# Two-layer MLP behind a 2-D Fourier transform: the tiles that TensorE reads are laid at one address modulo 256 bytes

## The chip, the cores and the metric

The kernel runs on one core of one Trainium2 chip. A core has five engines that run side by side: TensorE (matmuls, PE in the rows, and PEld for its weight loads), VectorE (DVE), ScalarE (ACT), GpSimd (POOL) and SyncE (SP, which issues the DMAs here). The metric is the device time of one execution in microseconds, lower is better. The on-chip memory that engines read their operands from is called SBUF here; an address is a byte offset within each of its 128 partitions.

## The reference

The reference takes the real part of a 2-D Fourier transform of each of 8 sequences (3008 x 256) and feeds every row to a two-layer network with a squared ReLU.

```python
X = np.fft.fft(x, axis=1)            # x: (8, 3008, 256)
X = np.fft.fft(X, axis=2)
attn = X.real.astype(np.float32)     # rows become 24064 tokens of 256
...
h = x @ w_in                         # 256 -> 2048
r = np.maximum(h, 0.0)
g = s * (r * r) + b
return (g @ w_out).astype(np.float32)  # 2048 -> 256
```

## The kernel before

The transform along the sequence is split into small cosine and sine transforms (L652), and the one along the features is folded into the first layer's weights at the start of the program. What is left as the bulk of the work are the two layers.

The tokens are cut into 8 sequences x 3 blocks (`su`, `blk`) of 502 columns (`NT`), each with a plus and a minus half, so that a tile which TensorE streams has two halves of 502 columns. The 2048 hidden features are cut into 16 chunks `j` of 128. One step is one `j` of one block; there are 8 x 3 x 16 = 384 of them.

Every operand is kept as a high and a low float32r part, and a product is formed from three matmuls (high x high, high x low, low x high):

- **First layer** (L823, function `first_layer`): for each half, three matmuls stream `spec_h`, `spec_l`, `spec_h` against the weights `wd_h`, `wd_h`, `wd_l`. That is 6 matmuls in a step, 2,304 in all.
- VectorE adds a rank-one term and forms sum and difference (L826 to L828), ScalarE squares and casts into `gh` (L842 to L844), and GpSimd (VectorE in some steps) writes the rest `gl = h - gh` (L848).
- **Second layer** (L865, function `second_layer`): for each half `pm`, 6 matmuls stream `gh` and `gl` against `wo_h` and `wo_l`, each for two groups of 128 outputs (`dh`). That is 12 matmuls in a step, 4,608 in all.

Each of these 6,912 matmuls has 128 rows of weights of its own to load. Both layers accumulate in PSUM; `finish` evacuates four banks once in a block.

The order of all this work on every engine is written out by hand, in the two strings `START` (first sequence) and `BATCH` (the other seven): `L` is a first-layer step, `S` a second-layer step, `l`, `v` and `o` are pieces of the next sequence's transform. `_in_order` ties each engine's instructions to that order.

Tiles come from pools, which lie one behind another in SBUF in the order in which they are opened; within a pool, tiles lie in the order in which their tags first appear. `Ring` hands out numbered tags in turn. The pool `const` holds the weights, the pool `read` all that TensorE streams in the two layers (`gl`, `gh`, `spec_l`, `spec_h`, three buffers each). The element lengths given to `tile` thus set the addresses. In the built program they are, in bytes (and modulo 256):

| tile | first byte | first half, modulo 256 | second half, modulo 256 |
|---|---|---|---|
| `wd_h`, `wd_l` | 16640, 33024 | 0 | 0 (8192 bytes on) |
| `wo_h`, `wo_l` | 49472, 65856 | 64 | weights of `j`, `dh` are 1024 and 512 bytes apart, so 64 throughout |
| `gl`, three buffers | 155520, 159616, 163712 | 128 | 96 (2016 bytes on) |
| `gh`, three buffers | 167808, 171904, 176000 | 128 | 96 (2016 bytes on) |
| `spec_l`, three buffers | 180160, 184256, 188352 | 192 | 152 (2008 bytes on) |
| `spec_h`, three buffers | 192704, 196800, 200896 | 192 | 152 (2008 bytes on) |

Some lengths are padded for the layout's sake: the last of the eight first input tiles by 16 elements, one of the `spec_l` buffers by 64.

Of the kernel before, what the change touches and what calls it, by code (L numbers as in the profile page):

```python
# [9 lines left out]
F32 = mybir.dt.float32  # L10
I32 = mybir.dt.int32
F32R = mybir.dt.float32r
# [3 lines left out]
P = 128  # L16
NB, S, D, FF = 8, 3008, 256, 2048
# [3 lines left out]
R = 96  # L21
G = 24
NL = 4 * G
NK = H + 2
NT = 502
NBLK = 3
NJ = FF // P
ENGINES = tuple(getattr(mybir.EngineType, e) for e in ("PE", "DVE", "Activation", "Pool", "SP"))
# [19 lines left out]
TILES = (4, 6, 5, 7, 0, 1, 2, 3)  # L48
# [220 lines left out]
def kernel(ctx: ExitStack, tc: tile.TileContext, xq, xn, dft, turn, feat, w_in, w_out, s, b, out):  # L269
    nc = tc.nc  # L270
# [3 lines left out]
    const = ctx.enter_context(tc.tile_pool(name="const", bufs=1))  # L274
    stage = Ring(ctx.enter_context(tc.tile_pool(name="stage", bufs=1)), 2)
    wst = Ring(ctx.enter_context(tc.tile_pool(name="wst", bufs=1)), 4)
    fold = ctx.enter_context(tc.tile_pool(name="fold", bufs=1))
    small = Ring(ctx.enter_context(tc.tile_pool(name="small", bufs=1)), 2)
    read = Ring(ctx.enter_context(tc.tile_pool(name="read", bufs=1)), 3)
    act = Ring(ctx.enter_context(tc.tile_pool(name="act", bufs=1)), 3)  # L280
    outp = Ring(ctx.enter_context(tc.tile_pool(name="outp", bufs=1)), 2)
    late = ctx.enter_context(tc.tile_pool(name="late", bufs=1))
# [6 lines left out]
    def two_banks():  # L289
        held = banks.take()  # L290
        return held, ps_ab.tile([P, 2, 512], F32, name="ab", tag=f"ab{held[0]}")
# [8 lines left out]
    sb_b = const.tile([P, 1], F32, name="sb_b")  # L300
    turn_sb = const.tile([R, 8], F32, name="turn_sb")
    bias = const.tile([P, 2], F32, name="bias")
    wd_h = const.tile([P, 2, FF], F32R, name="wd_h")
    wd_l = const.tile([P, 2, FF], F32R, name="wd_l")
    wny = const.tile([P, NJ], F32, name="wny")
    wo_h = const.tile([P, NJ, D], F32R, name="wo_h")
    wo_l = const.tile([P, NJ, D], F32R, name="wo_l")
    feat_sb = small.tile([P, 4 * P + 152], F32, name="feat_sb", tag="ebc")[:, :4 * P].rearrange("p (k n) -> p k n", k=2)
# [137 lines left out]
    def nyquist(ph, t, room):  # L446
# [64 lines left out]
        yield  # L511
        e = room if ph else outp.tile([P, 2 * NT], F32, name="e", tag="o")
        to = 0
# [17 lines left out]
    def block_of(su, blk):  # L531
        if (su, blk) not in spec_tiles:
            spec_tiles[su, blk] = [spec_part(part) for part in "hl"]
        return spec_tiles[su, blk]

    def spec_part(part, more=0):
        t = read.tile([P, 1024 + more], F32R, name=f"spec_{part}")
        return t[:, :2 * NT].rearrange("p (k n) -> p k n", k=2)

    folded = {}  # L540

# [75 lines left out]
    def store(su, ph, parts, low_engine=nc.gpsimd):  # L617

        pieces = []
        for r, o in parts:  # L620
            at, groups, size, kept = PLACES[ph][r]
            n = groups * kept
            first = at // NT
            if (at + n - 1) // NT == first:
                pieces.append((
                    first, at - first * NT, n, lambda v, g=groups: v.rearrange("p k (a g) -> p k a g", a=g),
                    o.rearrange("p k (a g) -> p k a g", a=groups)[:, :, :, :kept],
                ))
            else:
                cut = (first + 1) * NT - at  # L630
                pieces.append((first, NT - cut, cut, lambda v: v, o[:, :, :cut]))
# [184 lines left out]
    def first_layer(su, blk, j, ebc):  # L816
        mh, ml = block_of(su, blk)
        held, ps = two_banks()
        ps = ps[:, :, :NT]
        fj = slice(j * P, (j + 1) * P)  # L820
        for kind in range(2):
            for i, (w, m) in enumerate(((wd_h, mh), (wd_h, ml), (wd_l, mh))):
                nc.tensor.matmul(ps[:, kind], w[:, kind, fj], m[:, kind], start=i == 0, stop=i == 2)  # L823
        yield
        h = act.tile([P, 2, NT], F32, name="h")
        nc.vector.scalar_tensor_tensor(h[:, 0], ebc, wny[:, j:j + 1], ps[:, 0], op0=ALU.mult, op1=ALU.add)  # L826
        sub(h[:, 1], h[:, 0], ps[:, 1])  # L827
        add(h[:, 0], h[:, 0], ps[:, 1])  # L828
        banks.give(held)
        step = (su * NBLK + blk) * NJ + j  # L830
        rows = (slice(1, 2), slice(0, 1)) if step in HALVED else (slice(0, 2),)
        gh = read.tile([P, 2, NT + 2], F32R, name="gh")
        gl = read.tile([P, 2, NT + 2], F32R, name="gl")
        if (su, blk) == (0, 0):

            nc.gpsimd.memset(gh[:, 0, NT:].bitcast(F32), 1.0)
            nc.gpsimd.memset(gl[:, 0, NT:].bitcast(F32), 0.0)
        for pm in rows:
            if step in SQUARES_OF_STEPS_ON_VECTOR:
                nc.vector.scalar_tensor_tensor(h[:, pm], h[:, pm], 0.0, h[:, pm], op0=ALU.max, op1=ALU.mult)  # L840
            else:
                nc.scalar.activation(h[:, pm], h[:, pm], AF.Relu)  # L842
                nc.scalar.activation(h[:, pm], h[:, pm], AF.Square)  # L843
            nc.scalar.copy(gh[:, pm, :NT], h[:, pm])  # L844
        yield gh, gl
        engine = nc.vector if step in LOWS_OF_STEPS_ON_VECTOR else nc.gpsimd
        for pm in rows:
            engine.tensor_sub(gl[:, pm, :NT], h[:, pm], gh[:, pm, :NT].bitcast(F32))  # L848
        yield
# [20 lines left out]
    def finish(su, blk, po):  # L870
        if (su, blk) == (0, 0):
            for dh in range(2):
                nc.vector.tensor_scalar(bias[:, dh:dh + 1], po[dh][:, NT:NT + 1], sb_b, None, ALU.mult)
        last = (su, blk) == (NB - 1, NBLK - 1)
        for pm in range(2):
# [15 lines left out]
    tiles = {}  # L891
    for n, c in enumerate(TILES):
        pool, tag = ((stage, "xt"), (read, "gl"), (read, "gh"))[(n + 1) // 3]
        more = 16 if n == len(TILES) - 1 else 0
        t = pool.tile([R, 4 * D + more], F32, name="xt", tag=tag)
        tiles[c] = t[:, :4 * D].rearrange("p (q d) -> p q d", q=4)

    unit = read.tile([P, 1024], F32, name="unit", tag="spec_l")
    minus = unit[:R, 2 * R:6 * R].rearrange("p (i l) -> p i l", i=4)
    lo = [spec_part("l", 64 * k) for k in range(2)]  # L900
    room = read.tile([P, 1024], F32, name="room", tag="spec_h")
    hi = [spec_part("h") for _ in range(2)]
    for k in range(2):
        spec_tiles[0, k] = [hi[k], lo[k]]
# [49 lines left out]
    def load_e(n):  # L954
        su, blk = divmod(n, NBLK)
        ebc[n] = small.tile([P, NT], F32, name="ebc")
        for ph in range(2):
            first, last = max(0, blk * NT - SPLIT * ph), min((blk + 1) * NT - SPLIT * ph, e_dram[ph].shape[1])
            if first < last:
                at = first + SPLIT * ph - blk * NT  # L960
                nc.sync.dma_start(ebc[n][:, at:at + last - first], e_dram[ph][su, first:last].partition_broadcast(P))

    def first():
        nonlocal step
        su, blk, j = step // (NBLK * NJ), step // NJ % NBLK, step % NJ
        step += 1
        n = su * NBLK + blk
        if j == NJ // 2 + (NJ // 4 if n == 0 else 0) and n + 1 < NB * NBLK:
            load_e(n + 1)
        steps.append(((su, blk, j), first_layer(su, blk, j, ebc[n])))  # L970
        next(steps[-1][1])
# [93 lines left out]
```

## Time and profile before

| | |
|---|---|
| time, median of 3 runs | 1684.3 us (1683.22 to 1690.37) |
| span of the profiled execution, first to last instruction | 1682.0 us |
| TensorE busy in it | 1669.9 us (99%) |
| VectorE, ScalarE, GpSimd busy | 1279.8, 1243.3, 906.1 us |
| granted TensorE clock, mean | 1.000 |
| matmuls recorded | 7592, of which 6,912 at L823 and L865 |

The profiled execution's own time outside of the profiler isn't given; its span lies 2.3 us under the median of the runs, and 1.2 us under the fastest. Matmuls are pipelined: a matmul's recorded duration reaches to the end of its last column's way through the array, past the start of the next matmul. So the time that a matmul holds the engine is read from the distance between starts, and the recorded durations show where one differs from another.

### The profile page before, as it was taken

The page shows a single profiled execution, that of the slowest core. Times are in us where ns is not written, and L with a number is a line of the kernel's source. Part 1 is how long each engine was busy: PE and PEld are TensorE (multiplying, and loading weights), DVE is VectorE, ACT ScalarE, POOL GpSimd, SP SyncE. Part 2 cuts the span into 40 slices and gives each one's busy share as a digit, 9 for nine tenths or more (in the row PEclk, how much of TensorE's full clock was granted, in tenths as well). Part 3 has the DMA queues.
Part 4 walks back from the last instruction along what each step waited for, and adds up shares of the span by engine and source line. Part 5 has one row for each costly group of instructions (what it writes and reads, how often), then busy time and mean ns, then how long its engine had stood idle before and what let it go on. Part 6 is the DMA issues. An engine that isn't in the chain of part 4 may idle for free.

```text
span 1682.0 us, 21389 instructions
## 1 busy us (share of the span) xinstructions
PE 1669.9 (99%) x7592; PEld 1383.2 (82%) x7592; DVE 1279.8 (76%) x2010; ACT 1243.3 (74%) x1300; POOL 906.1 (54%) x538
## 2 busy tenths in 40 slices
PE   8999999999999999999999999999999999999999
PEld 5778888888888888888888888888888888888887
DVE  7998988976779867787687976788767886765453
ACT  4986766777777777767767777777778777687776
POOL 5664344555565555655555555555556555565554
PEclk9999999999999999999999999999999999999999
DMA  8211200210012100120000200012100110000000
GB/s 233 76 39 50 69 20 31 72 35 31 1 32 72 35 31 5 36 72 26 31 31 21 77 10 31 31 38 69 31 1 31 41 47 32 1 32 29 4 25 25
DMA packets 25680, 67.44 MB, mean 40 GB/s; under 512 B 4931, under 2 KB 10371, under 8 KB 25574
## 3 DMA queue, kind: packets, MB, share of 16 engines
q1 hardware_dynamic: 25574, 66.09, 12.9%
q8 instruction: 59, 0.97, 0.2%
q14 instruction: 47, 0.39, 0.1%
HBM read 41.35 MB, written 24.73 MB: 39 GB/s over the span
## 4 chain that ended last, share of the span: by engine, by line
PE 96%; DMA 2%; DVE 2%; issue 0%; SPq 0%; ACT 0%; DVEq 0%
PE po L865 62%; PE ab L823 31%; PE ab L652 3%; DMA raw<-in_w_in 1%; DMA xt<-in_xq 1%; PE ab L369 0%; DMA ebc<-e_dram 0%; DVE xt L557 0%; DVE h L826 0%; DVE h L827 0%; DVE h L828 0%; DVE cs L562 0%; DVE spec_l L638 0%; DVE o L724 0%; DVE wd_l L296 0%
## 5 line engine op out<-in xcount | busy, mean ns | idle before, releaser
L848 POOL TENSOR_TENSOR gl<-h,gh 128x1004 fp32r<-128x1004 f32 (+1 forms) x365 | 799.8, 2191 | 709.5 <-ACT gh L844 473.9
L842 ACT ACTIVATE h<-h 128x1004 f32<-128x1004 f32 (+1 forms) x380 | 395.4, 1041 | 352.6 <-DVE h L828 351.4
L826 DVE SCALAR_TENSOR_TENSOR h<-ebc,wny,ab 128x502 f32<-128x502 f32 x384 | 281.7, 734 | 327.0 <-PE ab L823 314.6
L865 PE MATMUL po<-gh,wo_h 128*128 128x502 f32 (+1 forms) x1536 | 477.1, 391 | 0.0
L865 PE MATMUL po<-gh,wo_l 128*128 128x502 f32 (+1 forms) x1536 | 475.3, 390 | 0.0
L865 PE MATMUL po<-gl,wo_h 128*128 128x502 f32 (+1 forms) x1536 | 473.7, 389 | 0.0
L844 ACT CAST gh<-h 128x1004 fp32r<-128x1004 f32 (+1 forms) x385 | 397.2, 1032 | 37.1 <-PE po L865 21.9
L843 ACT ACTIVATE h<-h 128x1004 f32<-128x1004 f32 (+1 forms) x380 | 396.2, 1043 | 12.1
L865 PEld LDWEIGHTS po<-gl,wo_h 128*128 128x128 f32 x1536 | 290.9, 189 | 60.4 <-POOL gl L848 0.4
L865 PEld LDWEIGHTS po<-gh,wo_l 128*128 128x128 f32 x1536 | 289.7, 189 | 58.9
L865 PEld LDWEIGHTS po<-gh,wo_h 128*128 128x128 f32 x1536 | 285.7, 188 | 54.7
L823 PE MATMUL ab<-spec_h,wd_h 128*128 128x502 f32 x768 | 301.6, 393 | 3.3 <-DVE h L828 2.5
L823 PE MATMUL ab<-spec_l,wd_h 128*128 128x502 f32 x768 | 298.8, 389 | 0.2 <-DVE spec_l L638 0.2
L823 PE MATMUL ab<-spec_h,wd_l 128*128 128x502 f32 x768 | 298.1, 388 | 0.0
L828 DVE TENSOR_TENSOR h<-h,ab 128x502 f32<-128x502 f32 x384 | 260.5, 679 | 13.2
L827 DVE TENSOR_TENSOR h<-h,ab 128x502 f32<-128x502 f32 x384 | 260.2, 678 | 13.3
L823 PEld LDWEIGHTS ab<-spec_h,wd_h 128*128 128x128 f32 x768 | 144.6, 188 | 34.8 <-DVE h L828 4.0
L823 PEld LDWEIGHTS ab<-spec_l,wd_h 128*128 128x128 f32 x768 | 146.1, 190 | 29.8 <-DVE spec_l L638 0.5
L823 PEld LDWEIGHTS ab<-spec_h,wd_l 128*128 128x128 f32 x768 | 144.2, 188 | 28.7
L884 DVE TENSOR_SCALAR o<-po,sb_s,bias 128x502 f32<-128x502 f32 x94 | 68.8, 795 | 9.4 <-PE po L865 9.4
L638 POOL TENSOR_TENSOR spec_l<-o,spec_h 128x384 fp32r<-128x384 f32 (+4 forms) x75 | 59.8, 814 | 18.4 <-ACT spec_h L635 17.3
L557 DVE TENSOR_TENSOR xt<-xt 96x512 f32<-96x512 f32 x56 | 59.3, 1058 | 0.0
(125 smaller groups left out, 727.4 us busy)
## 6 DMA issues: line engine op xcount, KB each, us to landing
xt<-in_xq SPq DMA_DIRECT2D x64, 384.0 KB
out<-o SPq DMA_DIRECT2D x46, 502.0 KB
raw<-in_w_in SPq DMA_DIRECT2D x8, 512.0 KB
raw<-in_w_out SPq DMA_DIRECT2D x8, 512.0 KB
ebc<-e_dram SPq DMA_DIRECT2D x16, 251.0 KB
ebc<-e_dram SPq DMA_DIRECT2D x8, 126.0 KB
out<-o SPq DMA_DIRECT2D x4, 251.0 KB
ebc<-e_dram SPq DMA_DIRECT2D x8, 125.0 KB
```

The lines of the kernel that those rows point to most:

```text
L557: add(t[:, 0::2], t[:, 0::2], t[:, 1::2])
L638: low_engine.tensor_sub(lo, src, hi.bitcast(F32))
L823: nc.tensor.matmul(ps[:, kind], w[:, kind, fj], m[:, kind], start=i == 0, stop=i == 2)
L826: nc.vector.scalar_tensor_tensor(h[:, 0], ebc, wny[:, j:j + 1], ps[:, 0], op0=ALU.mult, op1=ALU.add)
L827: sub(h[:, 1], h[:, 0], ps[:, 1])
L828: add(h[:, 0], h[:, 0], ps[:, 1])
L842: nc.scalar.activation(h[:, pm], h[:, pm], AF.Relu)
L843: nc.scalar.activation(h[:, pm], h[:, pm], AF.Square)
L844: nc.scalar.copy(gh[:, pm, :NT], h[:, pm])
L848: engine.tensor_sub(gl[:, pm, :NT], h[:, pm], gh[:, pm, :NT].bitcast(F32))
L865: nc.tensor.matmul(po[2 * pm + dh][:, :n], l[:, j, dh * P:(dh + 1) * P], r[:, pm, :n], start=start and first, stop=stop and last,)
L884: nc.vector.tensor_scalar(dst, src, *args, ALU.mult, ALU.add)
```

## The change

All weight tiles and all halves of streamed tiles get the same address modulo 256. Three things do it: the small tile `wny` (64 bytes) is placed ahead of `wd_h` and `wd_l` instead of behind them; the pool `read` is opened ahead of the pool `small`; and each tile of `read` is laid out as two halves of 512 elements, of which 502 (504 in the first block) are used, through one new function `halves_of`. The paddings go.

```diff
+HALF = 512
...
     fold = ctx.enter_context(tc.tile_pool(name="fold", bufs=1))
+    read = Ring(ctx.enter_context(tc.tile_pool(name="read", bufs=1)), 3)
     small = Ring(ctx.enter_context(tc.tile_pool(name="small", bufs=1)), 2)
-    read = Ring(ctx.enter_context(tc.tile_pool(name="read", bufs=1)), 3)
...
+    wny = const.tile([P, NJ], F32, name="wny")
     wd_h = const.tile([P, 2, FF], F32R, name="wd_h")
     wd_l = const.tile([P, 2, FF], F32R, name="wd_l")
-    wny = const.tile([P, NJ], F32, name="wny")
...
-    def spec_part(part, more=0):
-        t = read.tile([P, 1024 + more], F32R, name=f"spec_{part}")
-        return t[:, :2 * NT].rearrange("p (k n) -> p k n", k=2)
+    def halves_of(name):
+
+        return read.tile([P, 2, HALF], F32R, name=name)
+
+    def spec_part(part):
+        return halves_of(f"spec_{part}")[:, :, :NT]
...
-        gh = read.tile([P, 2, NT + 2], F32R, name="gh")
-        gl = read.tile([P, 2, NT + 2], F32R, name="gl")
+        gh, gl = halves_of("gh"), halves_of("gl")
...
-            nc.gpsimd.memset(gh[:, 0, NT:].bitcast(F32), 1.0)
-            nc.gpsimd.memset(gl[:, 0, NT:].bitcast(F32), 0.0)
+            nc.gpsimd.memset(gh[:, 0, NT:NT + 2].bitcast(F32), 1.0)
+            nc.gpsimd.memset(gl[:, 0, NT:NT + 2].bitcast(F32), 0.0)
...
-        more = 16 if n == len(TILES) - 1 else 0
-        t = pool.tile([R, 4 * D + more], F32, name="xt", tag=tag)
-        tiles[c] = t[:, :4 * D].rearrange("p (q d) -> p q d", q=4)
+        tiles[c] = pool.tile([R, 4, D], F32, name="xt", tag=tag)
...
-    lo = [spec_part("l", 64 * k) for k in range(2)]
+    lo = [spec_part("l") for _ in range(2)]
```

In the built program `wd_h` and `wd_l` then begin at 16704 and 33088, `wo_h` and `wo_l` stay, and the twelve buffers of `read` lie 4096 bytes apart from 142656 on: all have the residue 64, in both halves, since 2048 is a multiple of 256.

On every engine the same instructions stand in the same order as before, with the same shapes. Only a few rows that write pieces of `spec_h` and `spec_l` wait for other semaphores. On GpSimd (POOL), within the second half of the first sequence's work, these rows stood before (`spec_l` is written from `o` and `spec_h`, `gl` from `h` and `gh`; the brackets name the engines that a row waits for):

```order
L638 TENSOR_TENSOR spec_l<-o,spec_h 128x2x124 [waits Activation_49]
L638 TENSOR_TENSOR spec_l<-o,spec_h 128x2x68 [waits Activation_49]
L638 TENSOR_TENSOR spec_l<-o,spec_h 128x2x184 [waits Pool_49]
L848 TENSOR_TENSOR gl<-h,gh 128x2x502 [waits DVE_49,PE_49,Activation_49] x3
L848 TENSOR_TENSOR gl<-h,gh 128x2x502 [waits PE_49,DVE_49,Activation_49,Pool_49] x9
```

And at the same place of the changed kernel, whose lines have other numbers (L642 and L851 are the same two lines):

```order
L642 TENSOR_TENSOR spec_l<-o,spec_h 128x2x124 [waits Activation_49]
L642 TENSOR_TENSOR spec_l<-o,spec_h 128x2x68 [waits Activation_49]
L642 TENSOR_TENSOR spec_l<-o,spec_h 128x2x184 [waits Activation_49]
L851 TENSOR_TENSOR gl<-h,gh 128x2x502 [waits DVE_49,PE_49,Activation_49]
L851 TENSOR_TENSOR gl<-h,gh 128x2x502 [waits PE_49,DVE_49,Activation_49,Pool_49] x11
```

No row moved; the third waits for ScalarE instead of GpSimd's own earlier write, and two rows of `gl` have one more name in their list.

## Rows read from the trace of the kernel before

**Rows 1.** The page: span, busy time by engine, granted TensorE clock by slice.

```profile
span 1682.0 us, 21389 instructions
...
PE 1669.9 (99%) x7592; PEld 1383.2 (82%) x7592; DVE 1279.8 (76%) x2010; ACT 1243.3 (74%) x1300; POOL 906.1 (54%) x538
...
PEclk9999999999999999999999999999999999999999
```

**Rows 2.** The page: chain that ended last, shares by engine and line.

```profile
PE 96%; DMA 2%; DVE 2%; issue 0%; SPq 0%; ACT 0%; DVEq 0%
PE po L865 62%; PE ab L823 31%; PE ab L652 3%; DMA raw<-in_w_in 1%; DMA xt<-in_xq 1%; PE ab L369 0%; DMA ebc<-e_dram 0%; DVE xt L557 0%; DVE h L826 0%; DVE h L827 0%; DVE h L828 0%; DVE cs L562 0%; DVE spec_l L638 0%; DVE o L724 0%; DVE wd_l L296 0%
```

**Rows 3.** TensorE's matmuls by form: busy us, mean ns | idle before.

```profile
L865 PE MATMUL po<-gh,wo_h 128*128 128x502 f32 x1504 | 467.0, 391 | 0.0
L865 PE MATMUL po<-gh,wo_l 128*128 128x502 f32 x1504 | 465.4, 390 | 0.0
L865 PE MATMUL po<-gl,wo_h 128*128 128x502 f32 x1504 | 463.8, 389 | 0.0
L823 PE MATMUL ab<-spec_h,wd_h 128*128 128x502 f32 x768 | 301.6, 393 | 3.3 <-DVE h L828 2.5 <-DVE wd_l L296 0.8
L823 PE MATMUL ab<-spec_l,wd_h 128*128 128x502 f32 x768 | 298.8, 389 | 0.2 <-DVE spec_l L638 0.2
L823 PE MATMUL ab<-spec_h,wd_l 128*128 128x502 f32 x768 | 298.1, 388 | 0.0
```

**Rows 4.** TensorE in order of time, 698 to 712 us: start, us.

```profile
700.74 0.39 PE L823 MATMUL ab<-spec_h,wd_h 128*128 128x502 f32 x1
...
701.42 0.39 PE L823 MATMUL ab<-spec_h,wd_h 128*128 128x502 f32 x1
...
702.10 0.39 PE L823 MATMUL ab<-spec_h,wd_h 128*128 128x502 f32 x1
...
703.46 0.62 PE L865 MATMUL po<-gh,wo_h 128*128 128x502 f32 x2
...
704.82 0.61 PE L865 MATMUL po<-gh,wo_h 128*128 128x502 f32 x2
...
706.18 0.62 PE L865 MATMUL po<-gh,wo_h 128*128 128x502 f32 x2
```

**Rows 5.** Matmuls into po: duration ns min/median/max, first and last start.

```profile
L578 PE MATMUL po<-xt,unit x16: 379/379/379, 11.4 to 16.4; 96*96 96x256 f32 x16
...
L575 PE MATMUL po<-xt,unit x8: 592/592/641, 9.7 to 14.4; 96*96 96x512 f32 x8
```

**Rows 6.** Line L865: duration ns min/median/max; last, idle time by releaser.

```profile
L865 PE MATMUL po<-gh,wo_h x1536: 382/388/476, 51.2 to 1677.2; 128*128 128x502 f32 x185, 128*128 128x504 f32 x7
...
L865 PE MATMUL po<-gh,wo_l x1536: 383/392/397, 51.6 to 1677.4; 128*128 128x502 f32 x185, 128*128 128x504 f32 x7
...
L865 PE MATMUL po<-gl,wo_h x1536: 383/389/501, 52.1 to 1677.6; 128*128 128x502 f32 x185, 128*128 128x504 f32 x7
...
  POOL gl L848: 0.4, 1
```

**Rows 7.** Waits: engine and line waited for, us in total, times, longest.

```profile
POOL gl L848 <- ACT gh L844: 473.9, 255, 9.2
```

**Rows 8.** Windows of two second-layer steps: length, busy us of each engine, clock.

```profile
698.02:700.74 2.72, 2.72 (x14) 2.26 (x12) 2.38 (x4) 1.80 (x3) 2.22 (x4) 1.00 0.00 0
...
703.46:706.18 2.72, 2.72 (x14) 2.26 (x12) 2.62 (x5) 1.05 (x2) 2.18 (x1) 1.00 0.00 0
```

**Rows 9.** All engines in order of time at the end of the program.

```profile
1677.39 0.19 PEld L865 LDWEIGHTS po<-gl,wo_h 128*128 128x128 f32 x1
1677.62 0.39 PE L865 MATMUL po<-gl,wo_h 128*128 128x502 f32 x1
```

**Rows 10.** The chain in order of time, 690 to 720 us: start, us, what.

```profile
694.10 2.72 PE po L865 x12
...
703.62 5.46 PE po L865 x24
```

## Prediction

> **What bounds the kernel now.** I read the page first: TensorE is busy for 1669.9 us of a span of 1682.0 us, and the granted clock stands at full speed, the 2.4 GHz level, in all slices [rows 1]. The chain that ended last says the same from the other end: 96% of it is TensorE, 62% in the second layer (L865) and 31% in the first (L823) [rows 2]. So what the engine spends on one matmul, times 6,912 of them (4,608 at L865 and 2,304 at L823), is the kernel's time. VectorE, ScalarE and GpSimd have room (76, 74 and 54% busy, same group), and the weight load of the next matmul lies beside the running one.
>
> Then I asked what one matmul costs. By kind of matmul the means are 391, 390, 389, 393, 389 and 388 ns [rows 3], but these durations overlap: a matmul starts before the one ahead of it has drained. What counts is the distance of the starts, which the order of time shows. First-layer steps start at 700.74 and 702.10 with their second half at 701.42: 0.68 us for three matmuls. Second-layer steps: 703.46, second half 704.82, next step 706.18: 1.36 us for six [rows 4]. Both are 226.7 ns per matmul. Starts and durations thus differ by about 390 - 227 = 163 ns, the drain.
>
> Is 227 ns all streaming? The float32 matmuls of the start give a measure. They are recorded in two passes each, and a pass over 256 columns takes 379 ns without any spread, one over 512 columns 592 ns [rows 5]: 213 ns for 256 columns, 0.832 ns per column, and 379 - 213 = 166 ns of drain. If a float32r matmul moves its columns at twice the rate of such a pass (my assumption; 502 columns in 227 ns are faster than 0.832 ns each, so it must be well above the rate of a pass), 502 columns need 502 x 0.416 = 209 ns, and its duration would be 166 + 209 = 375 ns. Measured are 382 at the least, 388 to 392 in the middle and 397 at the most where nothing waited [rows 6]. So about 15 ns per matmul (390 - 375) are unexplained: 6,912 x 15 = 104 us. This is the whole stake of a change that moves addresses only.
>
> **The change, part by part.** *Instructions.* Every engine keeps its rows in the same order, and the number of DMAs is the same. No row of TensorE has another wait. A few rows at L635 and L638 wait for another semaphore, since two halves with a gap between them are told apart where one stretch was not; these rows stand on ScalarE and GpSimd (one on VectorE). GpSimd alone waits 473.9 us in all for ScalarE's casts [rows 7], and TensorE waited for GpSimd's output at L848 for 0.4 us in the whole run [rows 6]. Cost: nothing, under that cover of GpSimd idle time; without the cover a late spec_l would hold TensorE at L823, where that wait now ends 0.2 us of idle time [rows 3]. I take 0, with 0.4 us as the most.
>
> *Addresses of the other engines' tiles.* ScalarE, VectorE and GpSimd write gh, gl and the spec tiles at other places and with a gap of 40 or 32 bytes between the halves. The element counts stay. These engines' busy shares differ between two second-layer steps (ScalarE 1.80 against 1.05 us, VectorE 2.38 against 2.62), and TensorE needs 2.72 us for both [rows 8]. I take 0.
>
> *Addresses that TensorE reads.* By the program's layout the first layer's weights move from residue 0 to 64 (all residues are bytes modulo 256), the second layer's stay at 64. The streams stood at 192 (first half of spec, 152 the second, as 192 + 2008 = 2200 = 8 x 256 + 152) and at 128 (first half of gh and gl; 96 the second, 128 + 2016 = 2144 = 8 x 256 + 96). All go to 64. The distances from stream to weight were therefore 192, 152, 64 and 32, and become 0. The trace holds a test of distance: with 192 and 152 three matmuls need 0.68 us each time, with 64 and 32 six need 1.36 us [rows 4]. Four distances, one price: 226.7 ns. Two of the streams began at a multiple of 64 and two did not; that makes none either. Nor are the weights that load beside a stream what costs the 15 ns: the last matmul of all has no load behind it and takes 0.39 us as all others do [rows 9]. That row speaks against a collision of two readers whose distance one could choose.
>
> What the change does remove is change itself. Second-layer steps that follow a first-layer step take 2.72 us for twelve, but two in a row take 5.46 instead of 5.44 [rows 10]: the second of them costs 0.02 us more, though the addresses are the same ones in the same order. So a duration depends on what ran ahead. The order on TensorE has 69 second-layer steps right behind another. If equal addresses give every step the common price, 69 x 0.02 = 1.4 us are saved. The figures are rounded to 0.01 us, so the difference lies between 0.005 and 0.035 us and the saving between 0.3 and 2.4 us; I take 2.
>
> Bounds for the price that no row shows (distance 0): from below the duration without any excess, 375 ns, from above the longest undisturbed one, 397 ns. In time 390 - 375 = 15 ns gives -104 us, 397 - 390 = 7 ns gives +48 us. I take the common price, as the row it is nearest to: the unknown fifth distance is one of a kind with four that agree.
>
> **Rule against trace.** The Trainium skill, page "SBUF — State Buffer", section "Who interferes with whom", gives TensorE two read ports, one for the moving operand and one for weight loads, independent of each other, and says that it never waits on another engine. By that rule the distance of stream and weight can't matter and the sum would be 0 us; the trace agrees as far as its four distances go, and with the last matmul's 0.39 us.
>
> **The sum.** The profiled execution has a span of 1682.0 us, the median of three runs is 1684.3, so 2.3 us lie around the span or between executions. 1682.0 - 2 + 2.3 = 1682.3, and I write 1682 us.
>
> **Rivals.** *Short lock (faster).* With equal addresses each matmul meets the same state as the one before, so all may settle on one of the durations that today alternate. If it is the shortest, 382 to 383 ns, 6,912 x 7 = 48 us go: 1636 us; if half of them settle there, 1660 us. For it: the short ones exist in each second-layer group [rows 6]. Against it: nothing shows that what makes them short is an equal address.
>
> *No excess (much faster).* The 15 ns are all due to unequal residues, and go: 1684 - 104 = 1580 us. Against it: two streams with a 40-byte difference in distance cost the same. The skill's page "TensorE: Matmul & The Clock Gate", section "Back-to-back issue gap", has N / 2.4 + 2.5 ns between starts, 211.7 ns for 502 columns; by it 15 ns of the measured 226.7 would be excess and the time would also be about 1580 us. No run here shows that distance.
>
> *Long lock (slower).* The same settling, but on a long duration, above all in L865's second pair of matmuls, whose median is already 392 ns against 388 and 389 beside it. The place is every step of both layers. At 392 ns it costs 2 x 6,912 = 14 us: 1698 us; at the longest, 397, 48 us: 1732 us. It decides from 391.2 ns on (0.5% is 8.4 us, 1.2 ns per matmul). For it: the durations reach 397 where no one waits. That the halves are now alike would also end whatever short duration comes from stepping to another residue at a half's end.
>
> *Nothing at all* (the layout has no say) gives 1684 us and can't be told from my forecast.
>
> **How the numbers follow.** About 0.5% is what a measurement of this kernel can tell from no change. The forecast with *nothing at all* has 0.35 (1676 to 1692). Short lock has 0.30, spread from 1636 to 1676. No excess has 0.10. Long lock has 0.25, spread from 1692 to 1732, thinner towards its end. Faster is 0.30 + 0.10 = 0.40, same 0.35, slower 0.25. The range leaves out *no excess* (0.10) and the upper part of the long lock, about 0.08: 1636 to 1708 us. Since cases of both signs hold most of the chance, the forecast's own range is 1676 to 1692.
>
> **What would show it.** In the profile after, the starts of three first-layer matmuls should still lie 0.68 us apart and those of six second-layer ones 1.36, in both halves alike, with medians in all six groups near 389. A short lock shows medians of 382 to 385, a long lock 392 or more, no excess about 375, and in each the minimum and the median should close up, because every matmul is like the next. Two second-layer steps in a row should take 5.44 us. The prediction is wrong if the distance 0 is special, which no row of this trace can show; or if the moved tiles slow another engine so far that TensorE waits at L865 for gl.

## The result, and the profile after

The changed kernel takes 1664.6 us (median of 4 runs, 1662.23 to 1668.19) against 1683.8 us of the kernel before (4 runs beside it): a ratio of 0.9881, 95% interval 0.9858 to 0.9903. It is 1.2% faster. That lies in the wide range that the prediction drew around its rivals (1636 to 1708 us), but outside the one that it gave the forecast itself (1676 to 1692) and 17 us under its sum (1682). Of the rivals it is *short lock*, at a duration that was not its favourite one.

The page of the changed kernel, to be held against [rows 1, 2]: span, busy time by engine, clock, and the shares of the chain.

```profile
span 1663.8 us, 21402 instructions
...
PE 1647.9 (99%) x7592; PEld 1375.8 (83%) x7592; DVE 1291.8 (78%) x2010; ACT 1241.5 (75%) x1300; POOL 908.7 (55%) x538
...
PEclk9999999999999999999999999999999999999999
...
PE 92%; DVE 4%; DMA 2%; issue 1%; ACT 0%; POOLq 0%; SPq 0%; DVEq 0%
```

The span is 18.2 us shorter and TensorE's busy time 22.0 us. The clock stands at its upper level as before, so that is no part of it. The chain shows what is new beside the gain: TensorE's share fell from 96% to 92% and VectorE's rose from 2% to 4%.

TensorE's matmuls of the changed kernel by form (L868 is the old L865, L827 the old L823), as [rows 3]:

```profile
L868 PE MATMUL po<-gh,wo_h 128*128 128x502 f32 x1504 | 461.9, 388 | 0.0
L868 PE MATMUL po<-gh,wo_l 128*128 128x502 f32 x1504 | 458.4, 386 | 0.0
L868 PE MATMUL po<-gl,wo_h 128*128 128x502 f32 x1504 | 458.3, 385 | 0.2 <-POOL gl L851 0.2
L827 PE MATMUL ab<-spec_h,wd_h 128*128 128x502 f32 x768 | 299.5, 390 | 7.8 <-DVE h L832 6.9 <-DVE wd_l L297 0.8
L827 PE MATMUL ab<-spec_l,wd_h 128*128 128x502 f32 x768 | 296.2, 386 | 0.2 <-DVE spec_l L642 0.2
L827 PE MATMUL ab<-spec_h,wd_l 128*128 128x502 f32 x768 | 296.1, 386 | 0.0
```

All six means fell by 2 to 4 ns, and the idle time before the first group, on VectorE's `h`, went from 2.5 to 6.9 us. The durations of line L868 in the changed kernel (min/median/max), as [rows 6]:

```profile
L868 PE MATMUL po<-gh,wo_h x1536: 382/385/474, 50.6 to 1659.0; 128*128 128x502 f32 x185, 128*128 128x504 f32 x7
...
L868 PE MATMUL po<-gh,wo_l x1536: 382/385/396, 51.0 to 1659.2; 128*128 128x502 f32 x185, 128*128 128x504 f32 x7
...
L868 PE MATMUL po<-gl,wo_h x1536: 382/385/493, 51.5 to 1659.4; 128*128 128x502 f32 x185, 128*128 128x504 f32 x7
```

The medians 388, 392 and 389 became 385 each; the shortest, 382 or 383 before, are 382. Durations overlap, so the starts decide. TensorE of the changed kernel in order of time, as [rows 4]:

```profile
690.33 0.61 PE L868 MATMUL po<-gh,wo_h 128*128 128x502 f32 x2
...
691.67 0.61 PE L868 MATMUL po<-gh,wo_h 128*128 128x502 f32 x2
...
693.01 0.39 PE L827 MATMUL ab<-spec_h,wd_h 128*128 128x502 f32 x1
...
693.68 0.38 PE L827 MATMUL ab<-spec_h,wd_h 128*128 128x502 f32 x1
...
694.35 0.61 PE L868 MATMUL po<-gh,wo_h 128*128 128x502 f32 x2
```

Six second-layer matmuls now need 1.34 us (1.36 before) and three first-layer ones 0.67 (0.68). The chain of the changed kernel adds many of them up, as [rows 10] (start, us, what):

```profile
282.31 2.68 PE po L868 x12
285.00 1.34 PE ab L827 x6
...
342.25 5.36 PE po L868 x24
347.61 2.68 PE ab L827 x12
```

5.36 / 24 = 2.68 / 12 = 223.3 ns per matmul in both layers, against 226.7 (2.72 / 12) before. The accounts close: 6,912 x 3.33 ns = 23.0 us gained, 6.9 - 2.5 = 4.4 us given back to waits for `h`, 18.6 us net, and the span shows 18.2. The pieces are rounded to 0.01 us, so a price per matmul is good to about 0.4 ns for 12 and 0.2 ns for 24. Summed over all starts in the two traces, gaps of 260 ns and more left out, the mean distance went from 227.1 to 223.6 ns, which is 24 us for 6,912, and what those gaps last beyond the common price grew by 6.5 us: 18 us net again. (The idle times in the rows count from a matmul's recorded end, so they miss part of each gap.)

### The profile page after: what moved, and what is told of

Read it like the earlier page. It is cut to its first block, busy times and chain, and to the rows that moved or that the text cites. A ratio compares the mean times of both kernels' runs of the same rounds, so it can differ in the third digit from the quotient of the medians.

```text
span 1663.8 us, 21402 instructions
## 1 busy us (share of the span) xinstructions
PE 1647.9 (99%) x7592; PEld 1375.8 (83%) x7592; DVE 1291.8 (78%) x2010; ACT 1241.5 (75%) x1300; POOL 908.7 (55%) x538
## 4 chain that ended last, share of the span: by engine, by line
PE 92%; DVE 4%; DMA 2%; issue 1%; ACT 0%; POOLq 0%; SPq 0%; DVEq 0%
PE po L868 59%; PE ab L827 30%; PE ab L656 3%; DVE h L830 1%; DVE h L831 1%; DMA raw<-in_w_in 1%; DMA xt<-in_xq 1%; DVE h L832 1%; PE ab L370 0%; DVE cs L566 0%; DVE xt L561 0%; DMA dft_sb<-in_dft 0%; DMA room<-in_xn 0%; DVE xt L563 0%; DVE uv L403 0%
## 5 line engine op out<-in xcount | busy, mean ns | idle before, releaser
L851 POOL TENSOR_TENSOR gl<-h,gh 128x1004 fp32r<-128x1004 f32 (+1 forms) x365 | 801.7, 2197 | 689.8 <-ACT gh L847 485.0
L868 PE MATMUL po<-gh,wo_h 128*128 128x502 f32 (+1 forms) x1536 | 471.9, 388 | 0.0
L868 PE MATMUL po<-gl,wo_h 128*128 128x502 f32 (+1 forms) x1536 | 468.2, 386 | 0.2 <-POOL gl L851 0.2
L868 PE MATMUL po<-gh,wo_l 128*128 128x502 f32 (+1 forms) x1536 | 468.4, 386 | 0.0
L868 PEld LDWEIGHTS po<-gl,wo_h 128*128 128x128 f32 x1536 | 288.3, 188 | 55.8 <-POOL gl L851 0.7
L868 PEld LDWEIGHTS po<-gh,wo_l 128*128 128x128 f32 x1536 | 288.4, 188 | 55.3
L868 PEld LDWEIGHTS po<-gh,wo_h 128*128 128x128 f32 x1536 | 285.2, 188 | 51.9
L827 PE MATMUL ab<-spec_h,wd_h 128*128 128x502 f32 x768 | 299.5, 390 | 7.8 <-DVE h L832 6.9
L827 PE MATMUL ab<-spec_l,wd_h 128*128 128x502 f32 x768 | 296.2, 386 | 0.2 <-DVE spec_l L642 0.2
L827 PE MATMUL ab<-spec_h,wd_l 128*128 128x502 f32 x768 | 296.1, 386 | 0.0
L832 DVE TENSOR_TENSOR h<-h,ab 128x502 f32<-128x502 f32 x384 | 260.4, 678 | 13.3
L827 PEld LDWEIGHTS ab<-spec_h,wd_h 128*128 128x128 f32 x768 | 144.2, 188 | 40.0 <-DVE h L832 11.3
L827 PEld LDWEIGHTS ab<-spec_h,wd_l 128*128 128x128 f32 x768 | 144.1, 188 | 27.7
L827 PEld LDWEIGHTS ab<-spec_l,wd_h 128*128 128x128 f32 x768 | 144.2, 188 | 26.8 <-DVE spec_l L642 0.5
L642 POOL TENSOR_TENSOR spec_l<-o,spec_h 128x384 fp32r<-128x384 f32 (+4 forms) x75 | 60.3, 828 | 18.6 <-ACT spec_h L639 18.1
L561 DVE TENSOR_TENSOR xt<-xt 96x512 f32<-96x512 f32 x56 | 65.1, 1163 | 0.0
```

The lines of the kernel that those rows point to most:

```text
L561: add(t[:, 0::2], t[:, 0::2], t[:, 1::2])
L642: low_engine.tensor_sub(lo, src, hi.bitcast(F32))
L868: nc.tensor.matmul(po[2 * pm + dh][:, :n], l[:, j, dh * P:(dh + 1) * P], r[:, pm, :n], start=start and first, stop=stop and last,)
```

## The experiments

The theories, by the letters that the expectations use: **A**, the distance between a streamed tile and its weights must be 0 modulo 256; **A2**, the same with 512 as the modulus; **B**, it is enough that both halves of a tile are alike; **C**, each distance has a price of its own; **D**, the residue 64 itself matters, not the distance. Distances are stream minus weight in bytes, modulo 256. The diffs are against the changed kernel unless another is named; a padding changes addresses alone, no instruction. (The changed kernel itself has 13 semaphore instructions more than the kernel before, 12 on GpSimd and one on ScalarE; the padded kernels have them too, fast and slow ones alike, so they aren't what makes it faster.) This table sums up the layouts that the runs below measure; the last two columns are pieces of each kernel's chain (24 second-layer matmuls, and 12 first-layer ones), in us.

| layout | distance | time, us | ratio to before | 24 at `po` | 12 at `ab` |
|---|---|---|---|---|---|
| before | 192, 152, 64, 32 | 1683.8 | 1 | 5.46 | 2.72 |
| halves alike | 192 and 64 | 1683.9 | 0.9994 [0.9985, 1.0004] | 5.44 | 2.73 |
| changed | 0, residue 64 | 1664.6 | 0.9881 [0.9858, 0.9903] | 5.36 | 2.68 |
| all at residue 0 | 0, residue 0 | 1663.7 | 0.9880 [0.9864, 0.9896] | 5.36 | 2.68 |
| padded by 256 | 256 | 1665.6 | 0.9891 [0.9876, 0.9905] | 5.36 | 2.68 |
| padded by 64 | 64 | 1682.8 | 0.9994 [0.9985, 1.0003] | 5.44 | 2.72 |
| padded by 128 | 128 | 1682.6 | 0.9990 [0.9980, 0.9999] | 5.44 | 2.72 |
| padded by 224 | 224 | 1684.3 | 0.9998 [0.9989, 1.0007] | 5.44 | 2.72 |
| padded by 32 | 32 | 1689.1 | 1.0024 [1.0013, 1.0034] | 5.47 | 2.74 |

**One part alone: the halves.** The kernel before with the halves 2048 bytes apart, at the old places of the tiles (diff against before):

```diff
-        return t[:, :2 * NT].rearrange("p (k n) -> p k n", k=2)
+        return t[:, :2 * HALF].rearrange("p (k n) -> p k n", k=2)[:, :, :NT]
-        gh = read.tile([P, 2, NT + 2], F32R, name="gh")
-        gl = read.tile([P, 2, NT + 2], F32R, name="gl")
+        gh = read.tile([P, 2, HALF], F32R, name="gh")
+        gl = read.tile([P, 2, HALF], F32R, name="gl")
```

> The kernel before with one part of the change: halves lie 2048 bytes apart, so both halves of a tile have one residue modulo 256 (spec 192 against weights at 0, gh and gl 128 against weights at 64); pools and paddings as before. Theory A (the distance of stream and weight has to be 0 modulo 256): no gain, 1676 to 1690 us, medians at 388 to 392 ns. Theory B (it is enough that the residue doesn't change from one matmul to the next): all of the gain, 1660 to 1668 us, medians at 385 ns. Theory C (each distance has its own price): somewhere else, and the two layers differ.

No change: 1683.85 us. B falls. Two second-layer steps in a row take 5.44 instead of 5.46 us here, twice 2.72, so that small extra did go with unequal halves; it can't be seen in the time, also because 12 first-layer matmuls take mostly 2.73 us here instead of 2.72.

**Another residue, the same distance.** 192 bytes ahead of the weights, so that weights and streams all stand at residue 0:

```diff
+    const.tile([P, 48], F32, name="pad_w")
     wd_h = const.tile([P, 2, FF], F32R, name="wd_h")
```

> The changed kernel with everything that TensorE reads moved by 192 bytes: streams and weights at residue 0 instead of 64, distances still 0. Theories A and B: as the changed kernel, 1660 to 1668 us and medians at 385 ns. Theory D (the residue 64 itself matters, where a stream begins within a 256-byte row): another time, by more than 5 us.

1663.69 us, as fast as the changed kernel. D falls; the distance is what counts.

**Everything alike, but at a distance of 64.** All streams move 64 bytes on, weights stay:

```diff
+    ctx.enter_context(tc.tile_pool(name="gap", bufs=1)).tile([P, 16], F32, name="pad_r")
     read = Ring(ctx.enter_context(tc.tile_pool(name="read", bufs=1)), 3)
```

> The changed kernel with the streamed tiles 64 bytes further on: every distance 64 modulo 256, halves still alike. Theory A: the gain is gone, 1676 us or more, medians at 388 ns or more. Theory B: 1660 to 1668 us. Theory C: a price of its own; before, steps with distances 64 and 32 took 1.36 us for six, so about that.

The whole gain is gone: 1682.76 us. Of this kernel, two pieces of its chain, and the durations at the second layer (min/median/max), as [rows 6]:

```profile
293.99 2.72 PE ab L828 x12
296.71 5.44 PE po L869 x24
```

```profile
L869 PE MATMUL po<-gh,wo_h x1536: 382/392/477, 51.0 to 1676.1; 128*128 128x502 f32 x185, 128*128 128x504 f32 x7
```

The median is 392 instead of 385. That every matmul meets the same state as the one ahead of it, which was my reason for a lock, is thus not enough: here all is uniform as well, and it is slow.

**A distance of 128.** As above with 32 elements.

> As the run before with 128 bytes: every distance 128 modulo 256, the farthest there is. Theory A: gain gone, 1676 us or more. Theory B: 1660 to 1668 us. Theory C: a price of its own; if stream and weights collide in rows of 256 bytes, the farthest distance should be the best or the worst of all.

1682.6 us, the price of 64.

**A distance of 256.** As above with 64 elements.

> The changed kernel with the streamed tiles 256 bytes further on: residues modulo 256 as in the changed kernel (distance 0), modulo 512 the distance is now 256. In the changed kernel all distances are 0 modulo 512 as well. Theory A (modulo 256 is what counts): 1660 to 1668 us, medians 385 to 386 ns. Theory A2 (the true modulus is 512 or more): the gain is gone, 1680 to 1686 us.

1665.57 us, and this kernel's chain has the short pieces:

```profile
296.56 5.36 PE po L869 x24
...
347.54 2.68 PE ab L828 x12
```

256 is as good as 0. A2 falls, A holds.

**Distances of 32 and 224.** As above with 8 and with 56 elements.

> The changed kernel with the streamed tiles 32 bytes further on: distance 32 modulo 256. If distance 0 is one point: 1680 to 1686 us as with 64 and 128. If it is the bottom of a valley some tens of bytes wide: between, some 1668 to 1676 us.

> The changed kernel with the streamed tiles 32 bytes ahead of their residue (224 bytes further on): distance 224, or -32, modulo 256. One point: 1680 to 1686 us. A valley: as with 32, or, if the weights' reading starts a little behind the stream's and an offset makes up for it, lower than with 0, under 1660 us, on one of the two sides.

With 32 the time is 1689.1 us, 0.24% longer than before, with 224 (which is 32 to the other side) 1684.33, no change. So C holds in part: distances other than 0 are not all alike, and the sign matters. 1689.1 us lies outside what either case expected for 32, and no valley shows on either side. In the chain of the kernel with 32 the longer price is seen in both layers:

```profile
292.58 2.74 PE ab L828 x12
295.32 5.47 PE po L869 x24
```

**The first layer alone at distance 0.** `gh` and `gl` 64 bytes on, the `spec` tiles, which lie behind them, another 192:

```diff
+    ctx.enter_context(tc.tile_pool(name="gap", bufs=1)).tile([P, 16], F32, name="pad_r")
...
-        tiles[c] = pool.tile([R, 4, D], F32, name="xt", tag=tag)
+        more = 48 if n == len(TILES) - 1 else 0
+        tiles[c] = pool.tile([R, 4 * D + more], F32, name="xt", tag=tag)[:, :4 * D].rearrange("p (q d) -> p q d", q=4)
```

> The changed kernel with gh and gl 64 bytes further on and the spec tiles left at residue 64: distance 0 in the first layer (2,304 matmuls), 64 in the second (4,608). If each matmul's price hangs on its own distance: a third of the gain, some 1676 to 1679 us, with medians of 385 to 386 ns in the first layer and 389 to 392 in the second. If the price hangs on the whole stream of matmuls being alike: no gain, 1680 to 1686 us.

1679.76 us (1678.93 to 1680.24), ratio 0.9969 [0.9958, 0.9981]: 5 us of some 19, a quarter instead of the third that was expected, and just above the expected 1676 to 1679. Its chain:

```profile
319.77 2.74 PE po L869 x12
322.51 2.69 PE ab L828 x12
325.20 5.44 PE po L869 x24
```

The layer that was laid at 0 got nearly the short price (2.69 against 2.68) and the other kept the long one: the price goes with the layer's own operands, not with the whole program being alike. What ran ahead has a say too: a second-layer step with first-layer steps on both sides takes 2.74 us here instead of 2.72, and that takes part of the first layer's gain away. The run also answers another doubt. A padding ahead of `read` moves the pools behind it as well; here they stand 256 bytes on, at the residues of the changed kernel, and the second layer still pays.

**An offset of 16 bytes.** The first layer at a distance of +16, the second at -16:

```diff
+    ctx.enter_context(tc.tile_pool(name="gap", bufs=1)).tile([P, 56], F32, name="pad_r")
...
-        return read.tile([P, 2, HALF], F32R, name=name)
+        return read.tile([P, 2, HALF], F32R, name=name)[:, :, 4:]
...
-        tiles[c] = pool.tile([R, 4, D], F32, name="xt", tag=tag)
+        more = 8 if n == len(TILES) - 1 else 0
+        tiles[c] = pool.tile([R, 4 * D + more], F32, name="xt", tag=tag)[:, :4 * D].rearrange("p (q d) -> p q d", q=4)
```

> The changed kernel with the first layer's streams 16 bytes behind the residue of the weights (distance +16) and the second layer's 16 bytes ahead of it (distance -16). If only exact equality pays: about 1680 to 1688 us, medians 389 ns or more in both layers. If memory is read in units of 32 bytes or more, so that 16 bytes stay in the same unit on one side: that side keeps medians of 385 to 386 ns and the other loses them; by the count of matmuls a gain kept in the first layer alone gives some 1679 us and one kept in the second alone some 1670 us.

1710.64 us (1709.29 to 1715.52), ratio 1.0172 [1.0155, 1.0189]: the slowest of all, and far from both cases of the expectation. Of this kernel, the chain and the durations at the second layer:

```profile
287.08 2.77 PE po L869 x12
...
294.91 2.74 PE ab L828 x12
297.65 5.57 PE po L869 x24
```

```profile
L869 PE MATMUL po<-gh,wo_h x1536: 384/392/473, 50.6 to 1702.8; 128*128 128x502 f32 x185, 128*128 128x504 f32 x7
...
L869 PE MATMUL po<-gh,wo_l x1536: 387/397/397, 51.0 to 1703.1; 128*128 128x502 f32 x185, 128*128 128x504 f32 x7
```

At -16 a second-layer matmul needs 5.57 / 24 = 232.1 ns in two steps in a row, the first of them 2.77 / 12 = 230.8 ns as the row with 12 shows and so the second 2.80 / 12 = 233.3; and a median of 397 ns is what I had called the *long lock*: it exists, at another distance. At +16 the first layer pays 2.74 / 12 = 228.3 ns on average. The average hides a pattern: by the starts in the trace its six matmuls take about 229, 222, 229, 235, 224 and 233 ns in turn, though all six have the same distance. So the distance sets the price of a step; it is not the same price for each matmul in it.

Streams began here at odd multiples of 16 bytes, so the run alone can't tell the distance from that. What speaks against it is the kernel before, where the `spec` streams' second halves began at residue 152, which is no multiple of 16 at all, at the common price [rows 4]. No run here separates the two.

**One of the two second-layer weights off.** `wo_l` alone moved by 64 bytes, all else at distance 0:

```diff
+    ctx.enter_context(tc.tile_pool(name="gap", bufs=1)).tile([P, 48], F32, name="pad_r")
...
+    const.tile([P, 16], F32, name="pad_l")
     wo_l = const.tile([P, NJ, D], F32R, name="wo_l")
```

> The changed kernel with wo_l alone 64 bytes further on. A stream against wo_l then has distance -64 to its own weights (768 x 2 matmuls), while those that run while a tile of wo_l is loaded are the second one of gh against wo_h and the first one against wo_l. If the price hangs on a matmul's own weights: the group gh,wo_l moves to 389 to 392 ns, gh,wo_h stays at 385 to 386. If it hangs on the weights that load beside it: both groups move half way, means 387 to 389. In both cases about a quarter to a third of the gain is lost: 1668 to 1674 us.

1666.55 us (1666.34 to 1668.1), ratio 0.9902 [0.9888, 0.9917]. The means by form in this kernel, and below them its chain:

```profile
L870 PE MATMUL po<-gh,wo_h 128*128 128x502 f32 x1504 | 463.0, 389 | 0.0
L870 PE MATMUL po<-gh,wo_l 128*128 128x502 f32 x1504 | 462.1, 388 | 0.0
L870 PE MATMUL po<-gl,wo_h 128*128 128x502 f32 x1504 | 457.4, 385 | 0.2 <-POOL gl L853 0.2
L829 PE MATMUL ab<-spec_h,wd_h 128*128 128x502 f32 x768 | 299.4, 390 | 5.7 <-DVE h L834 4.9 <-DVE wd_l L298 0.7
```

```profile
294.76 5.39 PE po L870 x24
```

24 matmuls take 0.03 us longer than in the changed kernel. A third of the loss of 0.08 us that the distance 64 costs when all are off is 0.027: the price goes with the share of the pairs that are off, as far as figures rounded to 0.01 us can tell. By it 192 x 0.03 = 5.8 us (4,608 / 24 = 192) would be lost; the medians show 1.9 and the spans 2.5, less than I expected (1668 to 1674 us). In part that is because TensorE lost 2.0 us less to `h` (4.9 against 6.9), and the rest is within what the runs of the two kernels spread (1662 to 1668).

In duration two groups are longer, `gh,wo_l` and the one ahead of it, `gh,wo_h`, during which `wo_l` is being loaded: their medians are 389 and 388 ns, against 385 in the changed kernel and for `gl,wo_h` here. The trace, matmul by matmul, is sharper. Half a step has six matmuls, two of `gh,wo_h`, two of `gh,wo_l` and two of `gl,wo_h`; their medians are 385, 389, 389, 389, 383 and 385 ns. The second of `gh,wo_h` and both of `gh,wo_l` are longer. If the weights in use counted, it would be the two of `gh,wo_l`; if those that load beside the stream counted, the second of `gh,wo_h` and the first of `gh,wo_l`. Three are one more than either rule gives, so neither alone fits, and the run doesn't tell what does.

**What the faster TensorE ran into.** At one place the changed kernel's chain runs through VectorE:

```profile
301.99 1.35 PE ab L827 x6
303.43 0.75 DVE h L830
305.59 2.52 DVE xt L561
309.27 2.40 DVE cs L566
324.20 1.34 DVE xt L561
...
333.90 1.62 PE ab L827 x6
335.52 5.40 PE po L868 x24
```

VectorE forms `h` in the same queue as the additions of the next sequence's transform (L561 to L566), and some of these are stretched. VectorE and below it GpSimd of the changed kernel in order of time (start, us):

```profile
309.27 2.40 DVE L566 TENSOR_TENSOR cs<-xt 96x256 f32<-96x256 f32 x1
...
315.51 0.41 DVE L566 TENSOR_TENSOR cs<-xt 96x256 f32<-96x256 f32 x1
```

```profile
309.01 2.38 POOL L851 TENSOR_TENSOR gl<-h,gh 128x1004 fp32r<-128x1004 f32 x1 [1.45 <-DVE xt L563]
...
317.16 2.18 POOL L851 TENSOR_TENSOR gl<-h,gh 128x1004 fp32r<-128x1004 f32 x1 [5.77 <-ACT gh L847]
```

The same addition takes 0.41 us alone and 2.40 where GpSimd's `gl` had begun just ahead of it; it ends 0.28 us after that (309.01 + 2.38 = 311.39, 309.27 + 2.40 = 311.67). The Trainium skill, page "SBUF — State Buffer", section "Who interferes with whom", has a VectorE instruction with two inputs from SBUF contend with a GpSimd instruction that reads SBUF; these rows agree. In the whole trace of the changed kernel, the 43 of the 56 executions of L566 that had no work of GpSimd beside them took 0.41 to 0.42 us each. To test whether this is what the gain was given back to, VectorE gets less to do: three squares go to ScalarE and one `gl` to GpSimd.

```diff
-LOWS_OF_STEPS_ON_VECTOR = (6, 7, 8, 9, 13, 14, 15, 19, 23, 25, 29, 30, 34, 37, 39, 43, 44, 52, 53, 55)
-SQUARES_OF_STEPS_ON_VECTOR = (23, 26, 28, 45, 51)
+LOWS_OF_STEPS_ON_VECTOR = (6, 7, 8, 9, 13, 14, 15, 19, 23, 29, 30, 34, 37, 39, 43, 44, 52, 53, 55)
+SQUARES_OF_STEPS_ON_VECTOR = (23, 45)
```

> The changed kernel with three squares (steps 26, 28 and 51) and one low part (step 25) taken off VectorE and given to ScalarE and GpSimd. In the changed kernel TensorE waits for VectorE's line L832 in 19 places (18.1 us of idle time at L827) against 7 (6.5 us) before, most of them between 160 and 335 us. If VectorE's load in that stretch is what gives part of the gain back: 1659 to 1663 us, waits for L832 under 12 us. If the transform's own additions on VectorE make it late whatever else stands there: no change against the changed kernel.

1660.82 us (1660.42 to 1661.91), ratio 0.9867 [0.9853, 0.9882], the fastest of all. The groups by form and the chain's shares of this kernel:

```profile
L827 PE MATMUL ab<-spec_h,wd_h 128*128 128x502 f32 x768 | 299.0, 389 | 2.2 <-DVE h L832 1.7 <-DVE wd_l L297 0.3
```

```profile
PE 96%; DVE 2%; DMA 2%; issue 0%; ACT 0%; POOLq 0%; DVEq 0%
```

The waits for `h` fell from 6.9 to 1.7 us and the chain is again 96% TensorE. The gain over the changed kernel is 3.8 us by the medians and 4.5 by the spans. The two kernels' times weren't taken side by side and the intervals of their ratios overlap, but all four times of this one (1660.42 to 1661.91) lie under all four of the changed one (1662.23 to 1668.19). In the measure of the expectation, which counts the idle time of weight loads too, the waits for L832 fell from 18.1 to 6.0 us, under the 12 that it named.

**The same relief on the kernel before.** The same two lines, in the kernel before:

> The kernel before with the same four pieces of work (the squares of steps 26, 28 and 51 on ScalarE, the low parts of step 25 on GpSimd) taken from VectorE as in the version of the changed kernel that ran at 1660.8 us. Theory G (the waits for VectorE's h are what the faster TensorE ran into, and the relief pays because of the new layout): TensorE waited only 2.5 us for it before, so the relief brings 0 to 2 us, 1681.5 to 1684 us, ratio 0.9988 to 1.0. Rival H (the relief pays by itself, whatever the layout): the same 3.8 us as after, about 1680 us, ratio 0.9977. Rival I (the moved work makes GpSimd or ScalarE late where TensorE did not run into it before): 1685 us or more.

1684.05 us (1683.42 to 1685.8), ratio 0.9998 [0.9989, 1.0007]: nothing. Of this kernel, the group that waits for `h`:

```profile
L823 PE MATMUL ab<-spec_h,wd_h 128*128 128x502 f32 x768 | 301.7, 393 | 3.9 <-DVE h L828 3.1 <-DVE wd_l L296 0.7
```

G holds, H and I fall: the relief pays only with the new layout, where TensorE waits for `h`. A faster TensorE isn't the only way into that wait, though. The slowest kernel, with the offset of 16 bytes, has it too; its chain's shares:

```profile
PE 91%; DVE 7%; DMA 2%; issue 1%; SPq 0%; ACT 0%; DVEq 0%
```

It idles 4.6 us for `h`, against 4.9 in the fast kernel at residue 0 and 6.9 in the changed one. So a slower TensorE can meet VectorE's stretched additions as well; what the runs show is that in the changed kernel this wait cost about 4 us and that relieving VectorE gets them back.

## Why the prediction was right and where it was wrong, point by point

- **What bounds the kernel** was right: the price of one matmul on TensorE, 6,912 times. 3.33 ns less of it make 23.0 us, the gain before the waits.
- **The step that failed** is "I take the common price, as the row it is nearest to: the unknown fifth distance is one of a kind with four that agree." Four equal prices were taken for a law. They show that steps which mix the distances 192 and 152, or 64 and 32, cost about the same, and nothing of 0, the one value at which both addresses are alike. The runs show that 64, 128 and 224 share the price (5.44 us for 24), that 0 and 256 are cheaper (5.36), and that 32 (5.47) and -16 (5.57) are dearer; so 32, one of the four, isn't of a kind with the others once it stands alone. The rows were also too coarse for "one price": they are sums of three and six matmuls, and by the starts in the same trace single matmuls of the second layer took between 221 and 233 ns before, in a pattern that repeats from step to step.
- **The last matmul** as a witness against a collision of two readers failed too. With no load behind it, it takes 0.39 us in both kernels. At this rounding 385 and 389 ns can't be told apart, so the row had no say on a matter of 4 ns.
- **Short lock** is what came, with medians of 385 (I had named 382 to 385 as its sign), but the reason I gave for it fell: uniformity without distance 0 is slow (the run at 64). The prediction had held against it that nothing showed an equal address to be what makes a duration short; the runs at 0, 256 and 64 show that it is. That the time fell into the wide range is thus luck in part: the range was drawn around rivals of both signs, and the one that came true did so for another reason.
- **No excess** did not come. The estimate of 375 ns without any stall stays 10 ns below the median at distance 0; what the rest is, these runs don't show.
- **The instructions and the other engines' tiles** at no cost: right. TensorE waited 0.2 us of idle time for `gl`, ScalarE's and GpSimd's busy times moved by 1.8 and 2.6 us, and no order changed. VectorE's busy time rose by 12.0 us; in the equally fast kernel at residue 0 it rose by 1.8, so that isn't a price of the layout as such.
- **Two second-layer steps in a row** take 5.36 = 2 x 2.68 us: no extra 0.02, as forecast, though at another price than the 5.44 forecast. The 2 us set down for it are too small to be seen in the time, by the run with the halves alone.
- **Not foreseen** is the giving back: 4.4 us of waits for VectorE's `h`, in a chain that had shown 2% of VectorE.
- **Rule against trace.** The Trainium skill, page "SBUF — State Buffer", section "Who interferes with whom", has TensorE's two read ports independent, by which the distance would make 0 us. The measurement differs: with the same instructions the distance makes ratios from 0.9880 (all at residue 0) to 1.0024 (32), and 1.0172 with the offset of 16 bytes, and the measurement decides.

What stays open is the mechanism: that the distance modulo 256 between a layer's streams and weights sets the price of its steps is shown; whether it is the weights in use or those being loaded, how the price is shared among the matmuls of a step, and why 0 is the cheap value, isn't. The second layer alone at distance 0, other distances below 32, and an offset of +16 or of -16 bytes in both layers alike were not tried.

## What to carry to other kernels

Several equal prices at arbitrary values of a parameter say little about its one special value; where a layout can bring two operands that one engine reads together to equal addresses (here modulo 256 bytes), it is a padding and a run to find out. Where one engine's instruction price times its count is the time, 1.5% of that price can be worth more than all of that engine's waits in the trace. After such a gain, read the chain again: what was just hidden before (here VectorE's `h`, queued behind additions that GpSimd's work stretches) is the next few microseconds.

## What the runs showed of the hardware

- In a run of them, a float32r matmul of 128 x 128 weights and 502 streamed columns takes on average 223.3 ns from start to start at a distance of 0 or 256 bytes between stream and weights, 226.7 at 64, 128 and 224, 227.9 at 32, and in the run with the offset of 16 bytes 228.3 at +16 and 232.1 at -16. The granted clock was 0.997 to 1.000 in all of them, and the instructions were the same.
- The residue itself (0 or 64) makes no difference at distance 0: 1663.7 and 1664.6 us.
- The page "TensorE: Matmul & The Clock Gate" of the Trainium skill, section "Back-to-back issue gap", gives a gap of N / 2.4 + 2.5 ns, which is 211.7 ns for 502 columns, and calls it the gap of an isolated matmul. The runs here have float32r matmuls with a weight load each, and the nearest that one came to it is 223.3.
- An addition on VectorE of 96 x 256 elements takes 0.41 us, and 2.40 us where it begins 0.26 us behind a `gl` of 2.38 us on GpSimd.
